# The first batch's convolution and the place of its value products in a fused attention, gated-convolution and spatial-gating kernel

## Chip, cores and metric

One core of one Trainium2 chip runs the whole program in one launch. The metric is the device time of that launch in microseconds. Three runs of the kernel before took 686.89, 687.64 and 688.34 us (median 687.64).

## What is computed

Eight batches of 576 tokens pass through three layers. The core of the reference, shortened:

```python
# attention: 8 heads of 64; plain window of 32, or dilated by 4, in the second half of the heads
scores = np.where(masks, q @ k.T / 8, -1e9)
x = softmax(scores) @ v                       # batch x 576 x 512
...
# gated convolution over time, 5 taps per channel
gate_pre = sum(conv_w[k] * xp[:, k:k + S, :] for k in range(5))
x = (sigmoid(gate_pre) * (x @ w_val)) @ w_out
...
# spatial gating
h = np.maximum(x @ w_in, 0)                   # 512 -> 1024
u, v = h[..., :512], h[..., 512:]
v_s = einsum('ts,bsd->btd', w_spatial, layer_norm(v)) + b_spatial
out = (u * v_s) @ w_out2
```

## The kernel before

Channels lie on partitions, tokens on the free axis. Eight heads are four pairs of two; a pair gives one tile of 128 channels by 576 tokens. The scores of a pair are computed for the 32 by 64 blocks of the band alone (`a_scores`), then come the maximum (`a_max`), the exponentials on ScalarE (`a_exp`), the reciprocal of the sums (`a_sum`), the normalising and turning (`a_trans`), the values (`a_pv`), the convolution (`a_conv`) and its tanh (`a_tanh`). `mlp_steps` holds the rest of a batch: `val` (product with w_val, times the gate), `vstep` (v and its layer norm), `ustep`, `spstep` (spatial product) and `outstep`. The sigmoid is written as half of one plus a tanh.

Two products of weights are taken once: `fuse` multiplies the first layer's w_out (called wm) with the two halves of w_in (wiv for v, wiu for u), so that the middle matrix vanishes. Its products go to PSUM tiles, w_ps in the trace. The weights come as 64-bit words, and `from64` turns them into 32-bit floats with one ScalarE and four VectorE operations (L625, L626, L629, L632, L635). After the first batch most products are done in three passes over a high and a low part of each operand; `split` makes the parts, the high one by a ScalarE cast (L203), the low one by a GpSimd subtraction (L204).

The order of work before the first batch is a list written out by hand, `PRELUDE`. After it, events with places (`FIRST`, `mlp_steps`, `attention_events`) are sorted by place. A scheduler may still reorder within its rules; from the second batch on, TensorE's order is held by `keep_in_program_order`. The engines run their own orders and wait for each other by semaphores.

In the first batch the four pairs go through a path of their own. The block that `a_trans` turns is normalised by four GpSimd multiplications (L350, into `padded`, a part of the tile `boot`), turned by nine TensorE transposes (t_ps, L359) and copied by six ScalarE copies into `pt` (L362). `a_pv` multiplies with the values (o_ps), and ScalarE copies the result to `xt` (L397 or L399). The convolution of pairs 1 to 3 runs on VectorE (L424 and four times L426). That of pair 0 takes the branch at L416: ScalarE scales the five shifted copies (L418, L421), four of them into rotating `spare` tiles, and GpSimd adds them up (L422). ScalarE turns it into the tanh (L433). `val` of the first batch multiplies in one pass of 32-bit floats over four pairs, so each of its eight tiles needs all four `xt`; VectorE takes them out of PSUM (L481) and needs the tanh for that. Four PSUM buffers (`ps_m`) serve t_ps, w_ps and val_ps in turn.

Of the kernel before, what the change touches and what calls it, by code (L numbers as in the profile page):

```python
# [12 lines left out]
ACTF = mybir.ActivationFunctionType  # L13
ALU = mybir.AluOpType
AX = mybir.AxisListType

B, H, S, D = 8, 8, 576, 64
# [4 lines left out]
HS = S // 2  # L22
TAPS = 5
# [65 lines left out]
    ("w_f32", "wv", 1),  # L89
    ("load_w", "wiu", 1),  # L90
    ("a_trans", 0, 1),
    ("a_conv", 0, 0),
    ("fuse", "wiv", 2),
    ("fuse", "wiv", 3),
    ("a_max", 0, 3),
# [3 lines left out]
    ("a_trans", 0, 2),  # L99
    ("a_pv", 0, 2),  # L100
    ("a_trans", 0, 3),
    ("a_pv", 0, 3),
    ("fuse", "wiv", 1),
    ("a_tanh", 0, 0),
    ("a_conv", 0, 1),
    ("a_tanh", 0, 1),
# [40 lines left out]
def _f(ap):  # L147
    return ap.bitcast(F32)
# [3 lines left out]
def attention_gated_mlp_kernel(  # L152
# [15 lines left out]
    nc = tc.nc  # L168
# [13 lines left out]
    cw = const.tile([128, NC, TAPS], F32, name="cw")  # L182
# [6 lines left out]
    held = {}  # L189

    def weight(name):

        if name not in held:
            held[name] = wts.tile(LATE[name], F32R, tag=name, name=name)
        return held[name]

    def spare(name):
        t = rot.tile([128, DM, 2], I32, tag="raw", bufs=4, name=name)
        return _f(t).rearrange("p n w -> p (n w)")

    def split(raw, hi, lo):

        nc.scalar.copy(out=hi, in_=raw)  # L203
        nc.gpsimd.tensor_tensor(out=lo, in0=raw, in1=_f(hi), op=ALU.subtract)  # L204
# [3 lines left out]
    def matmul(o, a, r, start, stop):  # L208

        m = nc.tensor.matmul(o, a, r, start=start, stop=stop)  # L210
        if fixed:
            tc.keep_in_program_order(m)

    def products(o, pairs):
        for i, (a, r) in enumerate(pairs):
            matmul(o, a, r, i == 0, i == len(pairs) - 1)

    def cross(ah, al, bh, bl):
        return [(ah, bh), (ah, bl), (al, bh)]

    def half(i):
        return slice(i * HS, (i + 1) * HS)

    def chunk(c):
        return slice(c * 128, c * 128 + 128)
# [52 lines left out]
    def a_scores(b, p):  # L278
        t = qk_t.pop((b, p))
        s = ps_s.tile([128, 1024], F32, tag="s", name="s_ps")  # L280
        for i in range(2 * NS):
            x, e = divmod(i, 2)
            n = BLOCK[e][x]
            cols = slice(SW * x, SW * x + SW)
            keys = slice(QB * n, QB * n + SW)
            for h in range(2):
                r = slice(64 * h, 64 * h + 64)
                q = t[r, KEYS + QB * n:KEYS + QB * n + QB]
                o = 64 * e + QB * h
                matmul(s[o:o + QB, cols], q, t[r, keys], True, True)  # L290
        if b or p >= 2:
            load_qk(b, p + 2)
        s_t[b, p] = s
# [85 lines left out]
    def a_pv(b, p):  # L379
        u = vv_t.pop((b, p))  # L380
        if b == 0:
            xt = act.tile([128, 4 + S], F32, tag=f"xh{p}", name="xt")
            xh[b, p] = xt[:, 4:]
        else:
            xt = rot.tile([128, 4 + S], F32, tag="xt", name="xt")
        nc.gpsimd.memset(xt[:, 0:4], 0.0)
        o = ps_o.tile([128, 1024], F32, tag="o", name="o_ps")
        for j in range(NJ):
            c = 512 * (j // 3) + 96 * (j % 3)
            for h in range(2):  # L390
                r = slice(64 * h, 64 * h + 64)
                matmul(o[r, c:c + 96], u[:, j, r], pt[:, :, h, j], True, True)
        o = o.rearrange("p (a c) -> p a c", a=2)[:, :, 0:HS]
        if b or p >= 2:
            load_vv(b, p + 2)
        if p < 2:
            nc.scalar.copy(out=xt[:, 4:].rearrange("p (a c) -> p a c", a=2), in_=o)  # L397
        else:
            nc.scalar.copy(  # L399
                out=xt[:, 4:].rearrange("p (i a r) -> p a r i", a=2, r=2),  # L400
                in_=o.rearrange("p a (r i) -> p a r i", r=2),
            )
        x_t[b, p] = xt
# [8 lines left out]
    def a_conv(b, p):  # L412
        xt = x_t.pop((b, p))
        t = act.tile([128, S], F32, tag=f"tt{p}", name="tt")
        tt[b, p] = t
        if b == 0 and p == 0:  # L416

            nc.scalar.activation(out=t, in_=xt[:, 0:S], func=ACTF.Copy, scale=cw[:, p, 0:1])  # L418
            for k in range(1, TAPS):
                u = spare("tap")[:, 0:S]  # L420
                nc.scalar.activation(out=u, in_=xt[:, k:k + S], func=ACTF.Copy, scale=cw[:, p, k:k + 1])  # L421
                nc.gpsimd.tensor_tensor(out=t, in0=t, in1=u, op=ALU.add)  # L422
            return
        nc.vector.tensor_scalar(out=t, in0=xt[:, 0:S], scalar1=cw[:, p, 0:1], scalar2=None, op0=ALU.mult)  # L424
        for k in range(1, TAPS):
            nc.vector.scalar_tensor_tensor(  # L426
                out=t, in0=xt[:, k:k + S], scalar=cw[:, p, k:k + 1], in1=t, op0=ALU.mult, op1=ALU.add
            )
# [31 lines left out]
    def mlp_steps(b):  # L460
# [3 lines left out]
        def val(c, hf):  # L464
            if hf == 0:
                gh[c] = act.tile([128, S + 64], F32R, tag=f"gh{c}", name="gh")
                if c == 0:
                    low["g"] = act.tile([128, NC, S], F32R, tag="gl", name="gl")
            gl = low["g"][:, c]
            ps = ps_m.tile([128, 512], F32, tag="m", name="val_ps")  # L470
            cs, h = chunk(c), half(hf)
            pairs = []
            for e in range(NC):
                if b == 0:
                    pairs.append((wide["wv"][:, e, cs], xh[b, e][:, h]))
                else:
                    wh, wl = weight("wval_h")[:, e, cs], weight("wval_l")[:, e, cs]
                    pairs += cross(wh, wl, xh[b, e][:, h], xl[b][:, e, h])
            products(ps[:, 0:HS], pairs)
            t = tt[b, c][:, h]  # L480
            nc.vector.scalar_tensor_tensor(  # L481
                out=t, in0=t, scalar=1.0, in1=ps[:, 0:HS], op0=ALU.add, op1=ALU.mult
            )
            split(t, gh[c][:, h], gl[:, h])
            if hf == 1:
                nc.gpsimd.tensor_tensor(
                    out=gh[c][:, S:S + 64], in0=t[:, HS - 64:HS], in1=_f(gh[c][:, 512:S]), op=ALU.subtract
                )
# [93 lines left out]

        tiles = [(c, hf) for hf in range(2) for c in range(NC)]
        steps = [(val, c, hf) for c, hf in tiles] + [(vstep, i) for i in range(5)]
        for fn in (ustep, spstep, outstep):
            steps += [(fn, c, hf) for c, hf in tiles]
# [113 lines left out]
    def fuse(key, e):  # L700
# [28 lines left out]
        for fn in (  # L729
            load_qk, load_vv, load_mask, load_ident, load_bias, load_conv_w, load_w, load_sp, conv_w_f32, w_f32,  # L730
            split_pair, split_out, split_sp, fuse, a_scores, a_max, a_exp, a_sum, a_trans, a_pv, a_conv, a_tanh,
        )
    }
# [97 lines left out]
```

## Time and profile before

| | us |
|---|---|
| median of 3 runs | 687.64 (686.89 to 688.34) |
| the profiled execution | 686.94 |
| its span | 685.2 |
| TensorE busy in the span | 654.6 (96%) |
| VectorE busy | 437.1 (64%) |
| ScalarE busy | 291.4 (43%) |
| GpSimd busy | 331.3 (48%) |

The span is what the profiler saw of the program, 1.74 us less than the execution's own time. PE is TensorE's matmul, PEld its weight load, DVE VectorE, ACT ScalarE, POOL GpSimd, SPq the queue on which SyncE issues transfers. Times in the trace are us from the span's start. In a timeline a row gives the start, the length of a run of like instructions, the engine, the line and the tiles; in brackets stands how long the engine had been idle and which engine's work ended that. Matmuls of 32-bit floats appear as two passes each.

### The profile page before, as it was taken

The page shows a single profiled execution, that of the slowest core. Times are in us where ns is not written, and L with a number is a line of the kernel's source. Part 1 is how long each engine was busy: PE and PEld are TensorE (multiplying, and loading weights), DVE is VectorE, ACT ScalarE, POOL GpSimd, SP SyncE. Part 2 cuts the span into 40 slices and gives each one's busy share as a digit, 9 for nine tenths or more (in the row PEclk, how much of TensorE's full clock was granted, in tenths as well). Part 3 has the DMA queues.
Part 4 walks back from the last instruction along what each step waited for, and adds up shares of the span by engine and source line. Part 5 has one row for each costly group of instructions (what it writes and reads, how often), then busy time and mean ns, then how long its engine had stood idle before and what let it go on. Part 6 is the DMA issues. An engine that isn't in the chain of part 4 may idle for free.

```text
span 685.2 us, 16752 instructions
## 1 busy us (share of the span) xinstructions
PE 654.6 (96%) x6804; PEld 599.1 (87%) x6804; DVE 437.1 (64%) x744; ACT 291.4 (43%) x619; POOL 331.3 (48%) x370
## 2 busy tenths in 40 slices
PE   3699889989999999999999999999999999999998
PEld 3456668879899998999899998999899989999998
DVE  5998977984786566656686566656676477632510
ACT  4865356533353334443353334343444334442422
POOL 2675798473544355434545355343635255424420
PEclk9999999999999999999999999999999999999999
DMA  8960124422222431233222421233122411010002
GB/s 338 397 208 28 48 79 146 127 81 92 77 75 78 134 88 31 76 107 110 60 77 77 140 83 54 68 103 115 41 78 85 139 42 33 20 60 18 1 1 70
DMA packets 43553, 63.13 MB, mean 92 GB/s; under 512 B 16850, under 2 KB 32594, under 8 KB 42964
## 3 DMA queue, kind: packets, MB, share of 16 engines
q1 hardware_dynamic: 34260, 52.62, 24.3%
q10 hardware_dynamic: 9216, 9.44, 4.0%
q8 instruction: 54, 0.88, 0.6%
q14 instruction: 23, 0.19, 0.1%
HBM read 44.33 MB, written 9.44 MB: 78 GB/s over the span
## 4 chain that ended last, share of the span: by engine, by line
PE 75%; DVE 12%; POOL 4%; ACT 3%; issue 2%; SPq 2%; DMA 2%; DVEq 0%; POOLq 0%; ACTq 0%
PE sp_ps L210 15%; PE out_ps L210 15%; PE val_ps L210 13%; PE v_ps L210 11%; PE u_ps L210 11%; PE o_ps L210 4%; PE s_ps L210 4%; DVE tt L426 3%; SPq L377 1%; POOL boot L350 1%; POOL vl L537 1%; POOL tt L422 1%; DMA raw<-in_w_mid_t 1%; DVE mx L307 1%; DMA pt<-et 1%
## 5 line engine op out<-in xcount | busy, mean ns | idle before, releaser
L426 DVE SCALAR_TENSOR_TENSOR tt<-xt,cw,tt 128x576 f32<-128x576 f32 x124 | 124.7, 1006 | 1.3
L210 PE MATMUL sp_ps<-wsp_h,vh 128*128 128x288 f32 x320 | 93.7, 297 | 0.6 <-ACT ru L549 0.6
L204 POOL TENSOR_TENSOR gl<-tt,gh 128x288 fp32r<-128x288 f32 x64 | 57.6, 902 | 66.6 <-ACT gh L203 66.6
L204 POOL TENSOR_TENSOR g2l<-ru,g2h 128x288 fp32r<-128x288 f32 x64 | 53.6, 847 | 64.1 <-ACT g2h L203 64.1
L210 PE MATMUL out_ps<-g2h,wout_h 128*128 128x288 f32 x256 | 76.9, 301 | 2.3 <-DVE ru L568 2.1
L210 PE MATMUL u_ps<-gh,w_h 128*128 128x288 f32 x256 | 76.5, 299 | 0.8 <-ACT v_t L501 0.8
L210 PE MATMUL out_ps<-g2l,wout_h 128*128 128x288 f32 x256 | 75.7, 296 | 0.0
L210 PE MATMUL u_ps<-gl,w_h 128*128 128x288 f32 x256 | 75.5, 295 | 0.0
L210 PE MATMUL u_ps<-gh,w_l 128*128 128x288 f32 x256 | 75.5, 295 | 0.0
L210 PE MATMUL sp_ps<-wsp_l,vh 128*128 128x288 f32 x256 | 75.4, 294 | 0.0
L210 PE MATMUL sp_ps<-wsp_h,vl 128*128 128x288 f32 x256 | 75.4, 294 | 0.0
L210 PE MATMUL out_ps<-g2h,wout_l 128*128 128x288 f32 x256 | 74.9, 295 | 0.0
L204 POOL TENSOR_TENSOR xl<-xt,xh 128x576 fp32r<-128x576 f32 x28 | 50.3, 1796 | 48.2 <-ACT xh L203 48.2
L537 POOL TENSOR_TENSOR vl<-v_t,vh 128x512 fp32r<-128x512 f32 x32 | 41.4, 1294 | 52.2 <-ACT vh L528 52.2
L210 PE MATMUL val_ps<-xh,wval_h 128*128 128x288 f32 x224 | 66.5, 297 | 0.0
L210 PE MATMUL val_ps<-xh,wval_l 128*128 128x288 f32 x224 | 66.1, 295 | 0.0
L210 PE MATMUL val_ps<-xl,wval_h 128*128 128x288 f32 x224 | 65.9, 294 | 0.0
L210 PEld LDWEIGHTS sp_ps<-wsp_h,vh 128*128 128x128 f32 x320 | 60.1, 188 | 1.5 <-ACT ru L549 0.9
L210 PE MATMUL v_ps<-w_h,gh 128*128 128x512 f32 x160 | 59.8, 398 | 0.0
L210 PE MATMUL v_ps<-w_l,gh 128*128 128x512 f32 x160 | 59.2, 394 | 0.0
L203 ACT CAST gh<-tt 128x288 fp32r<-128x288 f32 x64 | 27.3, 429 | 74.0 <-DVE tt L481 72.9
L424 DVE TENSOR_SCALAR tt<-xt,cw 128x576 f32<-128x576 f32 x31 | 18.7, 605 | 60.6 <-ACT xt L399 50.2
(137 smaller groups left out, 1666.3 us busy)
## 6 DMA issues: line engine op xcount, KB each, us to landing
qk_t<-in_qk SPq DMA_DIRECT2D x30, 592.0 KB, 4.9
vv_t<-in_vv SPq DMA_DIRECT2D x30, 384.0 KB, 3.9
out<-ob ACTq DMA_DIRECT2D x64, 144.0 KB, 1.8
pt<-et SPq DMA_DIRECT2D x224, 24.0 KB, 1.8
raw<-in_w_in SPq DMA_DIRECT2D x4, 1024.0 KB, 8.0
pt<-et SPq DMA_DIRECT2D x224, 12.0 KB, 1.8
raw<-in_w_mid_t SPq DMA_DIRECT2D x2, 1024.0 KB, 6.0
raw<-in_w_val SPq DMA_DIRECT2D x2, 1024.0 KB, 13.8
```

The lines of the kernel that those rows point to most:

```text
L203: nc.scalar.copy(out=hi, in_=raw)
L204: nc.gpsimd.tensor_tensor(out=lo, in0=raw, in1=_f(hi), op=ALU.subtract)
L210: m = nc.tensor.matmul(o, a, r, start=start, stop=stop)
L307: nc.vector.tensor_reduce(out=mx[:, :, 0], in_=e, axis=AX.X, op=ALU.max)
L350: nc.gpsimd.tensor_tensor(out=padded[r, lo:hi, k:k + SW], in0=e[r, lo:hi], in1=sm[r, lo:hi].to_broadcast([64, hi - lo, SW]), op=ALU.mult,)
L377: nc.sync.dma_start(out=pt[k:k + 32, i, h, j:j + hi - lo], in_=t[r:r + 32, c, lo:hi])
L422: nc.gpsimd.tensor_tensor(out=t, in0=t, in1=u, op=ALU.add)
L424: nc.vector.tensor_scalar(out=t, in0=xt[:, 0:S], scalar1=cw[:, p, 0:1], scalar2=None, op0=ALU.mult)
L426: nc.vector.scalar_tensor_tensor(out=t, in0=xt[:, k:k + S], scalar=cw[:, p, k:k + 1], in1=t, op0=ALU.mult, op1=ALU.add)
L537: nc.gpsimd.tensor_tensor(out=low["v"][:, i], in0=v, in1=_f(h), op=ALU.subtract)
```

## The change

Three things. The call of `a_conv` for pair 0 of the first batch moves in `PRELUDE` from behind the second pair's transposes to behind the last pair's values, and the branch for ScalarE and GpSimd is gone, so that pair 0 is convolved on VectorE like the others. The last part of the fuse that serves v (`fuse` of wiv, 1) moves ahead of the last pair's values. And the first matmul of the first batch's first `val` tile is held in program order, behind the last pair's values. Line numbers behind the edit differ: what was L350 is L353, L424 and L426 are L419 and L421, L715 is L711.

```diff
@@ PRELUDE
     ("a_trans", 0, 1),
-    ("a_conv", 0, 0),
     ("fuse", "wiv", 2),
...
     ("a_trans", 0, 3),
+    ("fuse", "wiv", 1),
     ("a_pv", 0, 3),
-    ("fuse", "wiv", 1),
+    ("a_conv", 0, 0),
     ("a_tanh", 0, 0),
@@ matmul, products
+        return m
-    def products(o, pairs):
+    def products(o, pairs, held=False):
         for i, (a, r) in enumerate(pairs):
-            matmul(o, a, r, i == 0, i == len(pairs) - 1)
+            m = matmul(o, a, r, i == 0, i == len(pairs) - 1)
+            if held and i == 0:
+                tc.keep_in_program_order(m)
@@ a_conv
-        if b == 0 and p == 0:
-
-            nc.scalar.activation(out=t, in_=xt[:, 0:S], func=ACTF.Copy, scale=cw[:, p, 0:1])
-            for k in range(1, TAPS):
-                u = spare("tap")[:, 0:S]
-                nc.scalar.activation(out=u, in_=xt[:, k:k + S], func=ACTF.Copy, scale=cw[:, p, k:k + 1])
-                nc.gpsimd.tensor_tensor(out=t, in0=t, in1=u, op=ALU.add)
-            return
@@ val
-            products(ps[:, 0:HS], pairs)
+
+            products(ps[:, 0:HS], pairs, held=b == 0 and c == 0 and hf == 0)
```

The built programs show what this makes of each engine's order. On TensorE, at the end of the fuse for v (w_ps), the last pair's values (o_ps) and the first batch's products (val_ps), the difference reads:

```order
 L210 MATMUL w_ps<-wiv_f_116,wm_f_264 128x512 x4
-L210 MATMUL val_ps<-xt,wv_f_206 128x288 x6
 L210 MATMUL o_ps<-pt,qkv 64x96 x12
-L210 MATMUL val_ps<-xt,wv_f_206 128x288 x22
+L210 MATMUL val_ps<-xt,wv_f_206 128x288 x28
 L210 MATMUL s_ps<-qk_t 32x64 x36
```

Six products that stood between the fuse and the last values now stand behind the values, with the other 22.

On ScalarE, at the same place, between the last copies into `pt` and the last pair's `xt`, the order before:

```order
L362 COPY pt<-t_ps 128x2x96 x6
L433 ACTIVATE tt<-tt 128x576
L625 ACTIVATE wiu_f_688<-raw 128x1024 x2
L714 ACTIVATE w_h<-w_ps 128x512
L203 CAST wm_h<-wm_f_264 128x512 x4
L433 ACTIVATE tt<-tt 128x576
L399 COPY xt<-o_ps 128x4x144
```

and the order now:

```order
L365 COPY pt<-t_ps 128x2x96 x6
L621 ACTIVATE wiu_f_680<-raw 128x1024
L428 ACTIVATE tt<-tt 128x576
L710 ACTIVATE w_h<-w_ps 128x512
L203 CAST wm_h<-wm_f_264 128x512 x4
L621 ACTIVATE wiu_f_680<-raw 128x1024
L402 COPY xt<-o_ps 128x4x144
```

One of the two conversions of wiu and the tanh of pair 2 have changed sides of the four casts of wm, and that tanh now stands behind the copy of `xt`; the evacuation of the fuse and the casts are ahead of the copy in both.

On VectorE, from the sum of pair 2 (sm) into the maximum of pair 3 (mx) and the conversion of w_val (wv_f), the order before:

```order
L335 TENSOR_SCALAR sm<-sm 128x9
L635 SCALAR_TENSOR_TENSOR wiv_f_116<-raw,wiv_f_116 128x1024
L336 RECIPROCAL sm<-sm 128x9
L303 TENSOR_TENSOR e_t<-s_ps,mask_sb 128x576
L307 TENSOR_REDUCE mx<-e_t 128x9
L309 TENSOR_SCALAR mx<-mx 128x9
L626 TENSOR_SCALAR wv_f_206<-wv_f_206 128x2x512
L629 TENSOR_SCALAR wv_f_206<-wv_f_206 128x2x512
L632 SCALAR_TENSOR_TENSOR wv_f_206<-raw,wv_f_206 128x2x512
L715 SCALAR_TENSOR_TENSOR w_l<-w_ps,w_h 128x512
```

and the order now:

```order
L338 TENSOR_SCALAR sm<-sm 128x9
L419 TENSOR_SCALAR tt<-xt,cw 128x576
L631 SCALAR_TENSOR_TENSOR wiv_f_116<-raw,wiv_f_116 128x1024
L339 RECIPROCAL sm<-sm 128x9
L306 TENSOR_TENSOR e_t<-s_ps,mask_sb 128x576
L421 SCALAR_TENSOR_TENSOR tt<-xt,cw,tt 128x576
L622 TENSOR_SCALAR wv_f_206<-wv_f_206 128x2x512
L310 TENSOR_REDUCE mx<-e_t 128x9
L421 SCALAR_TENSOR_TENSOR tt<-xt,cw,tt 128x576
L625 TENSOR_SCALAR wv_f_206<-wv_f_206 128x2x512
L312 TENSOR_SCALAR mx<-mx 128x9
L622 TENSOR_SCALAR wv_f_206<-wv_f_206 128x2x512
```

The five operations of pair 0's convolution are dealt out among these, three of them here and two more ahead of the reciprocal of pair 3.

On GpSimd, where the first batch's products are split (gl, gh) and the second batch's first pair is normalised (e_t), the order before:

```order
L204 TENSOR_TENSOR gl<-tt,gh 128x288
L486 TENSOR_TENSOR gh<-tt,gh 128x64
L338 TENSOR_TENSOR e_t<-e_t,sm 128x576
L204 TENSOR_TENSOR wiu_l<-wiu_f_688,wiu_h 128x512 x2
L204 TENSOR_TENSOR gl<-tt,gh 128x288
```

and the order now:

```order
L482 TENSOR_TENSOR gh<-tt,gh 128x64
L204 TENSOR_TENSOR wiu_l<-wiu_f_680,wiu_h 128x512
L341 TENSOR_TENSOR e_t<-e_t,sm 128x576
L204 TENSOR_TENSOR wiu_l<-wiu_f_680,wiu_h 128x512
L204 TENSOR_TENSOR gl<-tt,gh 128x288
```

One of the two subtractions of wiu now stands ahead of that normalisation, and one subtraction gl has gone behind both.

## Rows read from the trace of the kernel before

**Rows 1.** Windows: stretch, its length, busy us (instructions) by engine, TensorE's granted clock, DMA.

```profile
26.00:44.00 18.00, 14.19 (x133) 7.75 (x130) 17.83 (x18) 13.14 (x39) 12.75 (x10) 0.91 0.62 231
66.00:90.00 24.00, 20.18 (x216) 15.04 (x215) 19.28 (x30) 7.48 (x15) 18.38 (x19) 1.00 0.18 52
90.00:150.00 60.00, 55.64 (x572) 48.71 (x571) 52.70 (x83) 32.64 (x63) 43.24 (x38) 1.00 0.33 101
150.00:686.00 536.00, 531.35 (x5456) 504.05 (x5455) 311.04 (x560) 208.72 (x414) 236.72 (x277) 1.00 0.24 73
```

**Rows 2.** Timeline of TensorE: the last part of the fuse, products, last values.

```profile
50.27 3.60 PE L210 MATMUL w_ps<-wiv_f,wm_f 128*128 128x512 f32 x8
53.71 3.07 PE L210 MATMUL val_ps<-xt,wv_f 128*128 128x288 f32 x12
56.71 1.21 PE L210 MATMUL o_ps<-pt,qkv 128*64 128x96 f32 x24
```

**Rows 3.** Timeline of VectorE: the convolutions of pairs 1, 2 and 3.

```profile
46.75 1.06 DVE L424 TENSOR_SCALAR tt<-xt,cw 128x576 f32<-128x576 f32 x1
47.85 3.96 DVE L426 SCALAR_TENSOR_TENSOR tt<-xt,cw,tt 128x576 f32<-128x576 f32 x4
51.73 0.52 DVE L424 TENSOR_SCALAR tt<-xt,cw 128x576 f32<-128x576 f32 x1
52.28 3.38 DVE L426 SCALAR_TENSOR_TENSOR tt<-xt,cw,tt 128x576 f32<-128x576 f32 x4
...
59.22 0.60 DVE L424 TENSOR_SCALAR tt<-xt,cw 128x576 f32<-128x576 f32 x1 [2.96 <-ACT xt L399]
```

**Rows 4.** Timeline of ScalarE: taps of pair 0, then what surrounds the last copy.

```profile
27.54 2.76 ACT L421 ACTIVATE tap<-xt,cw 128x576 f32<-128x576 f32 x4
...
52.44 2.18 ACT L625 ACTIVATE wiu_f<-raw 128x1024 f32<-128x1024 f32 x2
54.52 0.58 ACT L714 ACTIVATE w_h<-w_ps 128x512 fp32r<-128x512 f32 x1
55.00 2.16 ACT L203 CAST wm_h<-wm_f 128x512 fp32r<-128x512 f32 x4
...
57.97 1.21 ACT L399 COPY xt<-o_ps 128x576 f32<-128x576 f32 x1 [0.22 <-PE o_ps L210]
...
73.74 1.15 ACT L203 CAST wiu_h<-wiu_f 128x512 fp32r<-128x512 f32 x2 [0.70 <-DVE wiu_f L635]
```

**Rows 5.** Tile wv_f (ns min/median/max, first and last start), then VectorE's timeline.

```profile
L626 DVE TENSOR_SCALAR wv_f<-wv_f x2: 685/1288/1890, 33.8 to 39.5; 128x1024 f32<-128x1024 f32 x2
L629 DVE TENSOR_SCALAR wv_f<-wv_f x2: 881/1328/1775, 34.5 to 41.4; 128x1024 int32<-128x1024 int32 x2
L632 DVE SCALAR_TENSOR_TENSOR wv_f<-raw,wv_f x2: 1224/1482/1739, 35.5 to 43.2; 128x1024 int32<-128x1024 int32 x2
L635 DVE SCALAR_TENSOR_TENSOR wv_f<-raw,wv_f x2: 1165/1498/1832, 37.7 to 45.1; 128x1024 int32<-128x1024 int32 x2
...
28.50 2.42 DVE L632 SCALAR_TENSOR_TENSOR wiv_f<-raw,wiv_f 128x1024 int32<-128x1024 int32 x1
...
44.95 0.20 DVE L336 RECIPROCAL sm<-sm 128x9 f32<-128x9 f32 x1
```

**Rows 6.** Timeline of GpSimd: pair 0's additions, multiplications of pair 2, the next batch.

```profile
28.44 1.40 POOL L422 TENSOR_TENSOR tt<-tt,tap 128x576 f32<-128x576 f32 x1 [0.95 <-ACT tap L421]
32.45 3.66 POOL L350 TENSOR_TENSOR boot<-e_t,sm 64x384 f32<-64x384 f32 x4 [2.61 <-DVE sm L336]
36.19 6.43 POOL L422 TENSOR_TENSOR tt<-tt,tap 128x576 f32<-128x576 f32 x3
...
74.73 1.15 POOL L338 TENSOR_TENSOR e_t<-e_t,sm 128x576 f32<-128x576 f32 x1
75.84 2.53 POOL L204 TENSOR_TENSOR wiu_l<-wiu_f,wiu_h 128x512 fp32r<-128x512 f32 x2
```

**Rows 7.** Waits of TensorE from 50 us on: us in total, times, longest.

```profile
PE w_ps L210 <- POOL wiu_l L204: 2.4, 2, 1.7
```

## The prediction, made before the changed kernel was run

> **What bounds the kernel now.** I read the windows first, because a gain is worth what it is worth where it falls. From 150 us to the end TensorE stands still for only 4.65 of 536 us [rows 1]: work that reaches that part on time cannot shorten it. Before it TensorE waits for others: 3.82 us in 66 to 90 and 4.36 us in 90 to 150. In 26 to 44 us, where the change puts its work, VectorE is busy 17.83 of 18.00 us [rows 1], so that stretch is VectorE's. So the time of the kernel is the time at which the first batch is let into TensorE's full part, and every term below is a shift of that moment.
>
> Then the timelines around the two edits. TensorE ends the fuse at 53.87, does 3.07 us of first products, and only then the last pair's values (o_ps, 56.71) [rows 2]. ScalarE copies these at 57.97, and VectorE, idle for 2.96 us, begins the last convolution at 59.22 [rows 3, 4]. That looks like a wait that the tie removes; term 2 shows why it mostly is not.
>
> **Term 1, the convolution of pair 0.** Out go five ScalarE operations (the four taps take 2.76 us [rows 4], under VectorE's stretch, so worth nothing) and four GpSimd additions. In come one tensor-scalar and four scalar-tensor-tensor operations on VectorE.
> *In:* pair 2's convolution, with GpSimd idle beside it, takes 0.52 + 3.38 = 3.9 us; pair 1's, beside GpSimd, 1.06 + 3.96 = 5.0 us [rows 3]. These are the ends.
> *Out:* while the additions run, VectorE's own operations are stretched. The conversion of wiv took 2.42 us beside the first addition [rows 5, 6]; the same operation on wv has a minimum of 1.22. Beside the other three (36.19 to 42.62 [rows 6]) the conversions of wv go from 0.69 to 1.89, 0.88 to 1.78 and 1.17 to 1.83 [rows 5]. The excess is 1.20 + 1.21 + 0.89 + 0.67 = 4.0 us. The fourth wv operation, 1.74 against 1.22, stands half beside the multiplications of pair 2, so 4.5 is the upper end.
> *Beside the multiplications:* these (32.45, 3.66 us [rows 6]) now meet pieces of the convolution. Between 3.9 and 5.0 I take half, +0.55: pair 1 has a similar four of them beside it, but here a PSUM read and a reduction stand among the pieces.
> *Order:* an operation that needs the one just before it starts 0.03 us after its end (51.73 + 0.52 to 52.28); an independent one 0.08 us before the end (47.85 + 3.96 to 51.73) [rows 3]. The pieces are now dealt out among the conversions and the maximum: nine neighbours stop depending on each other (four in the convolution, five in front), 9 x 0.11 = 1.0 us back; the lower end is none.
> Sum: 3.9 + 0.55 - 4.0 - 1.0 = -0.55 us, with ends of 5.0 - 4.0 = +1.0 and 3.9 - 4.5 - 1.0 = -1.6. This moves pair 3's reciprocal, today at 44.95 [rows 5], which lets GpSimd normalise the last pair, then TensorE transpose it and do the last fuse: all of the first batch hangs on it. The maximum of pair 3 itself comes later, since three pieces stand ahead of it; its exponentials on ScalarE then fall into time that ScalarE spends waiting, and end before the sum is wanted.
>
> The Trainium skill speaks against this edit: "Perfetto Trace Analysis", Optimizing Scalar/DVE Operations, advises moving work from a saturated VectorE to ScalarE or GpSimd. By that alone the term would be +3.9. The same section warns that GpSimd shares a read port with VectorE, and the stretched rows side with the warning.
>
> **Term 2, the tie.** It adds no instruction and no wait, it fixes a place in TensorE's order. The last pair's values leave TensorE 3.07 us earlier after the fuse. But ScalarE is in order, and ahead of their copy its program now has the fuse's evacuation (0.58), four casts of wm (2.16) and one of the two wiu conversions (2.18 for two) [rows 4], the casts waiting for the fuse. From the fuse's end at 53.87: 0.1 + 0.5 + 2.1 + 1.05 = 57.6 to 57.7 against 57.97 today, -0.3 us. So 2.8 of the 3.07 us are hidden behind ScalarE, and VectorE's idle time, 2.96 us, largely stays. The products lose nothing: the same passes run on TensorE, and their first evacuation still waits for the last convolution.
>
> **Term 3, what moves behind.** Together the last convolution begins 0.85 us earlier. Then GpSimd's order differs: one subtraction wiu_l (2.53 / 2 = 1.27 us) goes ahead of the normalisation e_t of the next batch's first pair [rows 6]. It must wait for its cast: today the first of two ends at 73.74 + 0.58 = 74.3 [rows 4]; one short evacuation of the products now stands behind the conversion instead of ahead of it, so about 74.0, and e_t starts near 75.25, not at 74.73: +0.5 on the chain over the transposed block, SP's sixteen small transfers and VectorE. For TensorE the same swap is a gain: its waits for wiu_l, 2.4 us in two [rows 7], lose about a third each way, 0.4 to 0.9. VectorE's chain comes out at -0.85 + 0.5 = -0.35, TensorE's own at about -1.2; what lies between 90 and 150 us follows sometimes one and sometimes the other. I take the middle, **-0.8 us**. SP's spatial loads no longer wait for the taps' buffers and go out earlier; the wiu loads wait for the same conversions as before. Both at nothing: the list of waits shows no engine that stands for either transfer in this stretch.
>
> The profiled execution took 686.94 us, so the sum is 686.1; the median of the runs shown is 0.70 above it, so I forecast **686.8**. Ends: the two of term 1 give 688.4 and 685.8 by the same sum. A measurement of this kernel tells about 0.2% (1.4 us) from no change.
>
> **Rivals.**
> 1. *TensorE's waits go as well (faster).* The statistics of the first v row and the wiu subtractions come earlier in the program. If all of the 2.4 us for wiu_l [rows 7] vanishes, and TensorE is not stopped again before 150, that is 2.4 in place of 0.65: -0.8 - 1.75, about 685.1. For it: 8.2 us of standing between 66 and 150 [rows 1], many chances. Against it: the chain over e_t and SP becomes later, not earlier, and most of the later waits end on VectorE.
> 2. *GpSimd's multiplications hold VectorE for their whole length (slower).* Place: 32 to 36 us. Today beside the four multiplications stand mostly operations that read PSUM or reduce, and VectorE's stretch there is only 0.52 + 0.20 (a tensor-scalar of 0.88 against 0.69). The change deals two tap operations into this place. If each multiplication stops VectorE wholly, the price is 3.66 - 0.72 = 2.9 in place of 0.55: term 1 becomes +1.8, the time 689.2. It decides from a reciprocal of pair 3 at about 46.5. For it: beside the first addition, begun 0.06 us before, VectorE lost 1.20 of the remaining 1.34 us [rows 5, 6]. Against it: the multiplications cover 64 partitions, and pair 1 lost only 1.1 us beside them. The Trainium skill ("SBUF — State Buffer", Who interferes with whom) says that the port pair is an exclusive lock, held for a whole instruction; the first addition agrees with it within 0.14 us.
> 3. *Nothing comes back (slower).* If the stretch in 36 to 43 us had another cause than the additions, all 3.9 us stay: about 690.8. The stretched rows begin and end with the additions, which speaks against it.
> 4. That the tie brings its whole 3.07 us is not a rival: ScalarE's order excludes it unless the casts leave.
>
> **How the numbers follow.** Forecast 0.45, rival 1 0.35, rival 2 0.16, rival 3 0.04. The forecast's own range is 685.8 to 688.4, of which the edge below 686.3 counts as faster, which is in rival 1's chance. The range over all cases reaches from just under rival 1, 684.8, to just over rival 2, 689.4; beyond are stronger forms of rival 1 and rival 3. Faster 0.35, same 0.45, slower 0.20.
>
> **What would show it.** Term 1: the conversions of wv near their minima, pair 3's reciprocal at 44 to 44.8 on VectorE. At 46.5 or later rival 2 holds. Term 2: o_ps directly behind the fuse, yet the copy behind the wm casts near 57.1, and a VectorE wait of 2 to 3 us before the last convolution at 58.4. If that wait is gone, term 2 was wrong. Term 3: e_t of the next batch not earlier than 74.4, and less of TensorE's wait for wiu_l. If TensorE stands less than 6 us between 66 and 150, rival 1 holds. After 150 both traces should take the same time; if not, the whole account is wrong.

## The result and the profile after

The changed kernel took 691.43 us (median of four runs, 690.35 to 692.18) against 687.67 for the kernel before (four runs, 686.89 to 688.34): ratio 1.0051, 95% interval [1.0031, 1.0070]. A second measurement gave 691.42 us and 1.0064 [1.0051, 1.0077]. It is slower, and outside the range of the prediction. The profiled execution took 691.45 us, its span is 689.7; TensorE is busy for 656.7 us, VectorE 440.4, ScalarE 289.6, GpSimd 321.7.

The windows of the changed kernel, for the stretches of [rows 1], and two short ones of 2 us (columns as there):

```profile
26.00:44.00 18.00, 14.66 (x99) 7.18 (x88) 18.00 (x26) 9.93 (x33) 4.85 (x6) 0.81 0.62 234
66.00:90.00 24.00, 19.37 (x213) 14.58 (x211) 18.58 (x30) 6.99 (x14) 16.55 (x19) 0.97 0.13 37
90.00:150.00 60.00, 55.14 (x498) 48.32 (x498) 52.14 (x76) 31.09 (x58) 41.00 (x36) 0.96 0.34 107
150.00:690.00 540.00, 535.10 (x5536) 507.41 (x5535) 315.44 (x568) 212.15 (x419) 239.15 (x281) 1.00 0.24 73
...
32.00:34.00 2.00, 2.00 (x3) 0.67 (x2) 2.00 (x4) 0.00 (x0) 1.93 (x3) 0.50 1.06 402
92.00:94.00 2.00, 2.00 (x6) 1.59 (x5) 1.83 (x4) 1.63 (x4) 1.85 (x2) 0.50 0.51 194
```

Behind 150 us nothing is lost: TensorE stands idle for 4.9 of 540 us, against 4.65 of 536 before. GpSimd lost the 8 us of additions in 26 to 44, as meant. The loss lies between, and one mark shows how much: the first product of the second batch's `val` starts at 161.5 us before and at 166.9 now, 5.4 us later, and from there to the end they need 523.6 and 522.7 us. The windows from 66 us to that mark, of the kernel before:

```profile
66.00:161.50 95.50, 87.23 (x888) 74.49 (x887) 80.08 (x124) 44.62 (x84) 67.29 (x62) 1.00 0.31 96
```

and of the changed kernel:

```profile
66.00:166.90 100.90, 89.96 (x893) 77.06 (x892) 82.90 (x125) 46.02 (x86) 65.62 (x63) 0.97 0.29 90
```

For the same matmuls, bar a few records, TensorE stands idle for 10.94 us in place of 8.27 (+2.7), and is busy for 2.7 us longer, at a granted clock of 0.97 in place of 1.00. So in these two profiles half of the 5.4 us is waiting and half is clock. (The profiled execution of before had a mean clock of 0.998, its other runs mostly 0.993; between medians the clock's part is smaller, see the last section.)

TensorE's timeline after, for [rows 2] (rows between left out):

```profile
31.32 11.79 PE L210 MATMUL w_ps<-wiv_f,wm_f 128*128 128x512 f32 x20 [2.98 <-DVE wiv_f L631]
44.18 0.87 PE L362 MATMUL t_ps<-ident_sb,boot 128*128 128x128 f32 x6
50.68 3.60 PE L210 MATMUL w_ps<-wiv_f,wm_f 128*128 128x512 f32 x8
54.21 1.21 PE L210 MATMUL o_ps<-pt,qkv 128*64 128x96 f32 x24
55.35 8.03 PE L210 MATMUL val_ps<-xt,wv_f 128*128 128x288 f32 x32
87.43 1.22 PE L210 MATMUL w_ps<-wiu_h,wm_h 128*128 128x512 f32 x4 [3.28 <-ACT wiu_h L203]
```

The tie does what it says: the last values (o_ps) follow the fuse at once, at 54.21 in place of 56.71. But the fuse's last part itself begins 0.41 us later than before.

VectorE's timeline after, for [rows 3, 5] and for what follows (rows between left out):

```profile
29.63 0.50 DVE L419 TENSOR_SCALAR tt<-xt,cw 128x576 f32<-128x576 f32 x1
31.93 1.07 DVE L421 SCALAR_TENSOR_TENSOR tt<-xt,cw,tt 128x576 f32<-128x576 f32 x1
34.50 1.19 DVE L421 SCALAR_TENSOR_TENSOR tt<-xt,cw,tt 128x576 f32<-128x576 f32 x1
36.89 0.80 DVE L421 SCALAR_TENSOR_TENSOR tt<-xt,cw,tt 128x576 f32<-128x576 f32 x1
39.95 0.81 DVE L421 SCALAR_TENSOR_TENSOR tt<-xt,cw,tt 128x576 f32<-128x576 f32 x1
43.62 0.20 DVE L339 RECIPROCAL sm<-sm 128x9 f32<-128x9 f32 x1
59.17 0.97 DVE L419 TENSOR_SCALAR tt<-xt,cw 128x576 f32<-128x576 f32 x1 [1.72 <-ACT xt L402]
60.18 4.27 DVE L421 SCALAR_TENSOR_TENSOR tt<-xt,cw,tt 128x576 f32<-128x576 f32 x4
64.37 1.18 DVE L477 SCALAR_TENSOR_TENSOR tt<-tt,val_ps 128x288 f32<-128x288 f32 x3
91.50 0.78 DVE L371 STREAM_TRANSPOSE et<-e_t 128x576 f32<-128x576 f32 x1 [4.65 <-POOL wiu_l L204]
98.32 2.48 DVE L711 SCALAR_TENSOR_TENSOR w_l<-w_ps,w_h 128x512 fp32r<-128x512 f32 x4 [0.37 <-ACT w_h L710]
110.07 0.69 DVE L508 BATCH_NORM_STATS2 st<-v_t 128x6 f32<-128x512 f32 x1 [0.31 <-ACT v_t L497]
```

The tile wv_f after, for the first four lines of [rows 5]:

```profile
L622 DVE TENSOR_SCALAR wv_f<-wv_f x2: 677/835/993, 32.9 to 36.3; 128x1024 f32<-128x1024 f32 x2
L625 DVE TENSOR_SCALAR wv_f<-wv_f x2: 679/680/680, 35.6 to 39.4; 128x1024 int32<-128x1024 int32 x2
L628 DVE SCALAR_TENSOR_TENSOR wv_f<-raw,wv_f x2: 1205/1206/1206, 38.2 to 42.5; 128x1024 int32<-128x1024 int32 x2
L631 DVE SCALAR_TENSOR_TENSOR wv_f<-raw,wv_f x2: 1209/1530/1852, 40.8 to 45.4; 128x1024 int32<-128x1024 int32 x2
```

The five pieces of pair 0's convolution take 0.50 + 1.07 + 1.19 + 0.80 + 0.81 = 4.37 us, the conversions are near their minima, and the reciprocal of pair 3 comes at 43.62 in place of 44.95. ScalarE after, for [rows 4], then GpSimd, for [rows 6] (rows between left out in both):

```profile
54.81 2.17 ACT L203 CAST wm_h<-wm_f 128x512 fp32r<-128x512 f32 x4
57.93 1.21 ACT L402 COPY xt<-o_ps 128x576 f32<-128x576 f32 x1
74.96 1.15 ACT L203 CAST wiu_h<-wiu_f 128x512 fp32r<-128x512 f32 x2 [1.98 <-DVE wiu_f L631]
```

```profile
31.56 3.51 POOL L353 TENSOR_TENSOR boot<-e_t,sm 64x384 f32<-64x384 f32 x4 [4.15 <-DVE sm L339]
45.29 4.63 POOL L353 TENSOR_TENSOR boot<-e_t,sm 64x384 f32<-64x384 f32 x4 [10.22 <-ACT pt L365]
75.66 1.30 POOL L204 TENSOR_TENSOR wiu_l<-wiu_f,wiu_h 128x512 fp32r<-128x512 f32 x1 [0.55 <-ACT wiu_h L203]
76.91 1.16 POOL L341 TENSOR_TENSOR e_t<-e_t,sm 128x576 f32<-128x576 f32 x1
```

GpSimd's second row is the one to look at: pair 3's multiplications wait 10.22 us, and not for the sum (the reciprocal ended at 43.82). The profile names ScalarE's copies into `pt`; these wait for pair 2's transposes (t_ps above, the first six done at 45.05), and the same transposes read the buffer that the multiplications overwrite. The row in the kernel before:

```profile
45.32 4.16 POOL L350 TENSOR_TENSOR boot<-e_t,sm 64x192 f32<-64x192 f32 x4 [2.70 <-ACT pt L362]
```

And the normalisation e_t of the next batch starts at 76.91 in place of 74.73. TensorE's list of waits from 50 us on:

```profile
PE w_ps L210 <- ACT wiu_h L203: 3.3, 1, 3.3
PE o_ps L210 <- DMA pt<-et: 3.0, 3, 2.2
```

The waits for wiu_l [rows 7] are gone; these two stand in their place.

### The profile page after: what moved, and what is told of

It is laid out like the page before. It is cut to its first block, busy times and chain, and to the rows that moved or that the text cites. A ratio compares the mean times of both kernels' runs of the same rounds, so it can differ in the third digit from the quotient of the medians.

```text
span 689.7 us, 16743 instructions
## 1 busy us (share of the span) xinstructions
PE 656.7 (95%) x6804; PEld 601.2 (87%) x6804; DVE 440.4 (64%) x749; ACT 289.6 (42%) x614; POOL 321.7 (47%) x366
## 4 chain that ended last, share of the span: by engine, by line
PE 84%; DVE 8%; ACT 2%; DMA 2%; POOL 2%; issue 1%; SPq 1%; DVEq 0%; POOLq 0%; ACTq 0%
PE sp_ps L210 15%; PE v_ps L210 15%; PE u_ps L210 14%; PE out_ps L210 14%; PE val_ps L210 13%; PE o_ps L210 5%; PE s_ps L210 4%; PE w_ps L210 3%; DVE tt L421 1%; POOL boot L353 1%; DMA raw<-in_w_mid_t 1%; SPq L380 1%; DVE wo_f L628 1%; DMA out<-ob 1%; DMA pt<-et 1%
## 5 line engine op out<-in xcount | busy, mean ns | idle before, releaser
L421 DVE SCALAR_TENSOR_TENSOR tt<-xt,cw,tt 128x576 f32<-128x576 f32 x128 | 130.6, 1022 | 1.2
L204 POOL TENSOR_TENSOR gl<-tt,gh 128x288 fp32r<-128x288 f32 x64 | 56.2, 882 | 68.2 <-ACT gh L203 68.0
L203 ACT CAST g2h<-ru 128x288 fp32r<-128x288 f32 x64 | 27.5, 431 | 70.0 <-DVE ru L564 69.7
```

What stands on the lines that cost most here:

```text
L421: nc.vector.scalar_tensor_tensor(out=t, in0=xt[:, k:k + S], scalar=cw[:, p, k:k + 1], in1=t, op0=ALU.mult, op1=ALU.add)
```

## Experiments

"Theory" in the quoted expectations is the account held when that kernel was run; it changed on the way, from the late normalisation to the order behind it.

### Each edit alone

**e1** leaves the tie out of the changed kernel (without it the fuse's new place in the list alters nothing), so what is left is the convolution on VectorE:

```diff
-            products(ps[:, 0:HS], pairs, held=b == 0 and c == 0 and hf == 0)
+            products(ps[:, 0:HS], pairs)
```

> The kernel before with only the convolution of pair 0 put on VectorE; the order of the fuse, the last values and the first products is that of before. Order theory (the loss comes from the order that the tie makes behind 55 us: the first evacuations after the whole last convolution, and wiu_l ahead of the next batch's normalisation e_t on GpSimd): pair 3's reciprocal near 43.6, e_t of the next batch near 74.5, time 686.9 to 687.9, ratio 0.999 to 1.000. Convolution theory (the five operations on VectorE are not paid back, rival 3 of the prediction): 690.5 to 691.5, ratio 1.004 or more. Clock theory (TensorE's lower granted clock in the fuse, which the earlier start of the fuse causes, costs the time): the fuse again takes about 11.8 us from 31.3, and the time is 688.5 to 690.

**e2** is the kernel before with the fuse ahead of the last values and the tie; pair 0 stays on ScalarE and GpSimd:

```diff
-    ("a_pv", 0, 3),
     ("fuse", "wiv", 1),
+    ("a_pv", 0, 3),
...
+            products(ps[:, 0:HS], pairs, held=b == 0 and c == 0 and hf == 0)
```

> The kernel before with only the fuse's last part ahead of the last values and the first product held behind them; pair 0 is convolved on ScalarE and GpSimd as before. GpSimd's order keeps e_t of the next batch ahead of both wiu_l. Order theory: e_t near 75 and no more, the first evacuations about 1 us later, time 687.5 to 689, ratio 1.000 to 1.002. If the tie costs by itself, whatever GpSimd's order: 690.5 to 691.5, ratio 1.004 or more. Convolution theory: 687.3 to 688, ratio 1.000.

| kernel | median us | ratio to before |
|---|---|---|
| e1, convolution alone | 687.41 | 0.9994 [0.9981, 1.0007] |
| e2, tie alone | 687.49 | 1.0001 [0.9989, 1.0013] |

Neither edit alone costs anything that shows within these intervals; together they cost 0.5 to 0.6%. So it is not VectorE's extra 4.4 us, and not the tie as such. The Trainium skill ("Perfetto Trace Analysis", Optimizing Scalar/DVE Operations) says that moving work from a saturated VectorE to ScalarE or even GpSimd may make sense; by that alone e1, which moves it back, would be slower. The interval says no change, which sides with that section's own warning on the port that GpSimd shares with VectorE.

### The late normalisation and the late copy

**e3** is the changed kernel with e_t held ahead of both subtractions wiu_l on GpSimd:

```diff
+    (4.605, ("split_pair", "wiu", 0)),
...
+            c, s = split(wide[key][:, m, 0:DM], hi, lo)
+            in_order(key == "wiu" and m == 0, s)
```

> The changed kernel with one order restored: on GpSimd the normalisation e_t of the next batch's first pair stands ahead of both subtractions wiu_l, as before. Order theory: e_t starts near 74.5 to 75.3 instead of 76.91, the shift of 2.2 us at e_t shrinks to under 0.7, TensorE's waits for the transposed block and for wiu_h shrink, time 688 to 689.5, ratio to before 1.001 to 1.003. Convolution theory, and late first evacuations alone: nothing comes back, 690.5 to 691.5, ratio 1.004 or more.

**e4** is the changed kernel with the four casts of wm held behind the last pair's copy on ScalarE:

```diff
+    ("split_pair", "wm", 0),
+    ("split_pair", "wm", 1),
...
+            in_order(key == "wm", c)
```

> The changed kernel with ScalarE's four casts of wm held behind the copy of the last pair's xt. On GpSimd e_t stands ahead of both wiu_l here too. Order theory, with term 2 of the prediction (the copy is held by the casts, not by the values): the copy starts near 55.8 instead of 57.93, the last convolution near 57.1 instead of 59.17, the first evacuation near 61.5 to 62.5, e_t near 72.5 to 73.5, time 685.5 to 687, ratio 0.997 to 0.999. Convolution theory: the 2.1 us come off 691.4, about 689.3, ratio 1.002. If another work then bounds the stretch (GpSimd's wm_l, now later), the copy is early and the time stays at 688 or more.

**e5** gives the kernel before what term 3 priced: one wiu_l ahead of e_t. **e9** puts both ahead. **e10** and **e11** do as e5 to the tie alone (e2) and the convolution alone (e1):

```diff
+    (4.59, ("split_one", "wiu", 0)),
+    (4.605, ("split_one", "wiu", 1)),
...
+            in_order(key == "wiu" and m == 1, s)
```

> The kernel before with nothing changed but GpSimd's order at 75 us: one subtraction wiu_l ahead of the next batch's normalisation e_t, the other behind it, as in the changed kernel. Order theory: e_t starts near 76 instead of 74.73 (1.27 us of one wiu_l, less 0.1 of slack), TensorE meets the late transposed block near 90, time 689 to 691, ratio 1.002 to 1.005. If the order at this place costs only its own 1.2 us: 688.5 to 689, ratio 1.0015 to 1.002. If the order is harmless and the changed kernel loses elsewhere: 687 to 688, ratio 1.000.

> As the run with one subtraction wiu_l ahead of the next batch's normalisation in the kernel before, but now both subtractions stand ahead of it: e_t starts near 77.3 instead of 74.73 and the second transposition of that batch near 92.4 to 92.6. If the lateness of e_t is what costs: another 1.2 us over the run with one, 689.5 to 690.5, ratio 1.0035 to 1.005. If the rest of the order that the scheduler makes with the swap costs, and not the lateness: 688.3 to 689.2, as with one, ratio 1.002 to 1.003.

> The tie alone (pair 0 still on ScalarE and GpSimd) with one subtraction wiu_l put ahead of e_t. The tie makes ScalarE's cast wiu_h 1.2 to 1.5 us late, and now e_t has to wait for it: e_t near 77.2 to 77.8. If lateness of e_t costs: 690 to 691.5, ratio 1.004 to 1.0055, with no convolution moved at all. If the changed kernel's loss needs its own order on VectorE behind 90 us: 688.5 to 689.5, ratio 1.002 to 1.003.

> The convolution alone on VectorE, with one subtraction wiu_l put ahead of e_t. wiu_h is not late here: e_t near 75.9. Lateness theory: 688.3 to 689, ratio 1.0015 to 1.0025. If the convolution adds to the loss once the order is disturbed: 690 or more, ratio over 1.004.

**e6** is the changed kernel again, beside e5, e7 and e8. **e7** is e4 with the four subtractions wm_l put off behind the first batch's first subtractions gl, **e8** with them later still:

```diff
+    (2.5, ("low_pair", "wm", 0)),
+    (3.2, ("low_pair", "wm", 1)),
...
+            if key == "wm":
+                in_order(True, nc.scalar.copy(out=hi, in_=wide[key][:, m, 0:DM]))
```

> The changed kernel once more, to see how often its TensorE falls to the lower clock and what that is worth. Order theory: every run is slower than before at the same mean granted clock, median 690.5 to 691.5, ratio 1.004 to 1.006, and runs at a mean clock of 0.995 or more still at 690 or above. Clock theory: the loss sits in the runs at a mean clock of 0.990 or under; runs at 0.995 or more take 687 to 688.5.

> The changed kernel with the casts of wm behind the copy of the last xt, and GpSimd's four subtractions wm_l held among the first subtractions gl instead of beside the last convolution; e_t ahead of both wiu_l. Contention theory (in the run with the copy alone, the convolution begun 3.2 us earlier was stretched from 3.4 to 7.09 us by wm_l): the last convolution takes 3.9 us from 56.0, the first evacuation starts near 60.5 instead of 63.6, and if wm_l then finds room on GpSimd e_t comes near 72 to 73.5 and the time is 685 to 686.5, ratio 0.996 to 0.998. If wm_l stretches the wiu conversions as it stretched the convolution: e_t near 74.5 to 75.5, time 687 to 688.5, ratio 0.999 to 1.001.

> As the run before this one, but wm_l stands still later on GpSimd, two subtractions each behind the sixth and the seventh pair of gl and gh, just ahead of e_t. Contention theory: the last convolution as there, first evacuation near 60.5; e_t then waits for 2.5 us of wm_l, near 74.5 to 76, and TensorE for wm_l near 78: time 687.5 to 690, ratio 1.000 to 1.003, worse than the run before this one by 1 to 3 us.

| kernel | e_t starts | median us | ratio to before |
|---|---|---|---|
| e3, normalisation first | 74.97 | 688.32 | 1.0007 [0.9996, 1.0018] |
| e4, copy first | 74.46 | 688.09 | 1.0006 [0.9992, 1.0019] |
| e5, before, one wiu_l ahead | 76.14 | 688.78 | 1.0023 [1.0014, 1.0032] |
| e9, before, both ahead | 77.28 | 690.06 | 1.0036 [1.0024, 1.0047] |
| e10, tie alone, one ahead | 76.39 | 689.16 | 1.0022 [1.0011, 1.0033] |
| e11, convolution alone, one ahead | 75.59 | 688.48 | 1.0005 [0.9993, 1.0017] |
| e6, changed kernel again | 77.03 | 691.42 | 1.0064 [1.0051, 1.0077] |
| e7, wm_l late | 74.95 | 690.29 | 1.0044 [1.0031, 1.0058] |
| e8, wm_l last | 77.03 | 689.77 | 1.0026 [1.0010, 1.0043] |

e3 and e4 each bring back nearly all of the loss, with e_t early in both; that alone would make the normalisation the culprit. The next rows forbid it. e7 has e_t as early as e3 and still costs 0.44%; e9 has it later than the changed kernel and costs less. And e8, expected to be worse than e7, is better.

Three cautions go with this table. Each start is that of one execution: e3 and e18 below are the same program, and e_t starts at 74.97 in one and at 74.19 in the other. The edit of e5 and e9 is not as small as it looks: counted in the traces as the least number of rows (by operation, tiles and shape) that must move to make one order of the other, the scheduler moved 35 rows of VectorE, 18 of ScalarE and 10 of GpSimd against the kernel before, and 35 or 36 of VectorE in e10 and e11 against e2 and e1. So their 0.05 to 0.36% is not the price of lateness alone; e12 below has that, with all else in e3's order: 0.16%, against 0.07% in e3. And e5 ran at a median granted clock of 0.988, the kernel before at 0.993; at the same clock it is not slower (last section).

e4 and e7 also settle term 2. VectorE's timeline of the last convolution in e4, with GpSimd's wm_l beside it (56.53 to 63.03):

```profile
56.00 0.52 DVE L420 TENSOR_SCALAR tt<-xt,cw 128x576 f32<-128x576 f32 x1 [1.06 <-ACT xt L403]
56.56 7.09 DVE L422 SCALAR_TENSOR_TENSOR tt<-xt,cw,tt 128x576 f32<-128x576 f32 x4
63.57 1.17 DVE L478 SCALAR_TENSOR_TENSOR tt<-tt,val_ps 128x288 f32<-128x288 f32 x3
```

and in e7, with GpSimd idle:

```profile
56.47 3.38 DVE L424 SCALAR_TENSOR_TENSOR tt<-xt,cw,tt 128x576 f32<-128x576 f32 x4
60.41 1.49 DVE L480 SCALAR_TENSOR_TENSOR tt<-tt,val_ps 128x288 f32<-128x288 f32 x3 [0.57 <-PE val_ps L213]
```

With the casts behind it the copy comes at 54.80 in e4, so the casts held it. But 3.7 us of the gain are stretched away again by the four subtractions, and the first evacuation (L478) comes at 63.57, against 63.18 before. The Trainium skill ("SBUF — State Buffer", Who interferes with whom) has VectorE and GpSimd contend for one port pair behind an exclusive lock; 7.09 against 3.38 us agrees that they contend. In e7 the evacuation comes at 60.41, 2.8 us earlier than before, and the kernel is slower all the same: what happens behind 82 us outweighs it.

### VectorE's order behind 82 us

What e7 shares with the changed kernel is VectorE's order there: in the traces 2 rows of VectorE stand elsewhere, while 26 do between the changed kernel and e3. So I wrote that order out as a list of places, forced without adding a wait:

```diff
+ORDER = [
+    89, 90, 91, 92, 102, 93, 99, 103, 94, 100, 104, 95, 101, 112, 113, 114,
...
+    for a, b in zip(ORDER, ORDER[1:]):
+        tc.add_manual_dep(
+            ranked[b], ranked[a].name,
+            mybir.DependencyInfo(mybir.DependencyClass.NoSync, mybir.DependencyReason.DATA),
```

**e12** is the changed kernel, its VectorE in e3's order from about 82 to 155 us; **e13** is e3 with the changed kernel's. The orders of the other engines were left to the scheduler, which moved them too.

> The changed kernel, wiu_l still ahead of e_t on GpSimd, but VectorE's operations from about 82 to 155 us are put into the order of the run e3 (64 places of that stretch differ). e_t near 76.9 as in the changed kernel. If the order on VectorE carries the rest of the loss: 689 to 690, ratio 1.0025 to 1.0035, what a late e_t alone costs. If lateness carries it all: 690.7 to 691.7, ratio 1.005 to 1.006, as in the changed kernel. If TensorE's clock carries it: a mean granted clock of 0.993 with the lower time, or 0.989 with the higher.

> The run e3 (e_t ahead of both wiu_l, near 75), but VectorE's operations from about 82 to 155 us in the order of the changed kernel. If the order on VectorE carries the rest of the loss: 689 to 690, ratio 1.002 to 1.0035, though e_t is early. If lateness carries it all: 688 to 688.6, ratio 1.0005 to 1.0015, as in the run e3.

**e14** to **e17** are e3 with the changed kernel's order in a part only: 82 to 115, behind 116, 82 to 88, and 95 to 115 us, by other lists; e14's part holds those of e16 and e17. **e18** is e3 with its own order written out, to see whether the writing itself costs anything.

> The run e3 with VectorE in the changed kernel's order from 82 to 115 us alone (the wiu conversions, the four evacuations w_l behind the reciprocal, the last taps ahead of the layer norm). If this front part costs: w_l four in a row from about 97.5, the first layer norm behind them near 105 to 106, first u_ps 1.5 to 2.5 us later than in e3, ratio 1.003 to 1.005. If the part behind 116 us costs: ratio 1.0005 to 1.0015.

> The run e3 with VectorE in the changed kernel's order behind 116 us alone (the third conversion of w_out ahead of the second group of evacuations ru). If this part costs: TensorE waits over 2 us more between 137 and 156 us, ratio 1.003 to 1.005. If the front part costs: ratio 1.0005 to 1.0015.

> The run e3 with the changed kernel's order on VectorE only from 82 to 88 us: layer norm of the first v row ahead of the last two wiu conversions, which end some 0.7 us later. If a late wiu_h for the second half of the fuse costs: TensorE's wait for it before 88 us grows by 0.5 to 1 us, ratio 1.0015 to 1.003. If the evacuations w_l cost: ratio 1.0005 to 1.0015.

> The run e3 with the changed kernel's order on VectorE only from 95 to 115 us: the four w_l in a row behind the sum and the reciprocal, the taps ahead of the layer norm. If these evacuations cost (they give TensorE its PSUM buffers back): first u_ps 1 to 2 us later than in e3, ratio 1.0025 to 1.0045. If not: ratio 1.0005 to 1.0015.

> The run e3 once more, with VectorE's order of 82 to 155 us written out as it already was: the same order on every engine. If e3 stands: ratio 1.000 to 1.0018. If its first measurement was lucky: 1.0025 or more, and then the four split runs lie within 0.2% of their base.

| kernel | first evacuation, e_t | median us | ratio to before |
|---|---|---|---|
| e12, changed, e3's order | 63.30, 75.86 | 688.36 | 1.0016 [1.0004, 1.0028] |
| e13, e3, the changed order | 64.86, 76.22 | 691.33 | 1.0047 [1.0032, 1.0062] |
| e14, the same to 115 us only | 63.51, 74.86 | 690.75 | 1.0050 [1.0037, 1.0064] |
| e15, the same behind 116 only | 64.18, 75.54 | 690.20 | 1.0045 [1.0027, 1.0062] |
| e16, the same in 82 to 88 only | 63.00, 74.34 | 689.73 | 1.0038 [1.0026, 1.0051] |
| e17, the same in 95 to 115 only | 62.63, 73.99 | 689.37 | 1.0037 [1.0023, 1.0051] |
| e18, e3 in its own order | 62.84, 74.19 | 687.73 | 1.0007 [0.9995, 1.0018] |

e12, e13 and e14 are the verdict between lateness and order: forcing VectorE's order takes most of the loss away, or brings most of it. e18 shows that forcing an order costs nothing by itself. e_t started at 75.86 in e12, where I had expected 76.9, and at 76.22 in e13, where e3 has 74.97. That came from further ahead, not from the forced rows: from the first evacuation to e_t it is 12.56 us in e12 and 12.54 in the changed kernel, 11.36 in e13 and in e3. e14 has an early e_t, 74.86, and the whole loss. From e_t to the mark of the second batch's `val` the kernel before, e1 to e4, e12 and e18 take 86.8 to 89.1 us, but the changed kernel 90.0 and (e6) 90.9, e13 91.0 and e14 91.5; part of that gap is clock, since the profiled executions of the first group ran at a mean of 0.992 to 0.998 and those of the second at 0.985 to 0.990.

What is not shown is that VectorE's order does it alone. The traces say how far the others went along: e12 is e3 on VectorE and ScalarE, row for row, with one row of GpSimd elsewhere, so 15 rows of ScalarE and 9 of GpSimd came back with VectorE's 26. In e13 VectorE's order is the changed kernel's, but 20 rows of ScalarE and 10 of GpSimd stand elsewhere than in e3, and 15 and 7 elsewhere than in the changed kernel. TensorE's order in the first batch moved too. And the parts don't add up: each of e14 to e17 costs 0.4 to 0.5% by itself. So no single exchange of rows is the whole cause.

What such an order does can be seen at the low parts w_l of the fuse for u. Each of these operations gives TensorE one of its PSUM buffers back. VectorE's timeline in e3:

```profile
89.77 0.78 DVE L373 STREAM_TRANSPOSE et<-e_t 128x576 f32<-128x576 f32 x1 [3.27 <-DMA pt<-et]
...
95.29 0.69 DVE L714 SCALAR_TENSOR_TENSOR w_l<-w_ps,w_h 128x512 fp32r<-128x512 f32 x1
96.19 1.28 DVE L714 SCALAR_TENSOR_TENSOR w_l<-w_ps,w_h 128x512 fp32r<-128x512 f32 x2
97.51 0.63 DVE L714 SCALAR_TENSOR_TENSOR w_l<-w_ps,w_h 128x512 fp32r<-128x512 f32 x1
...
105.75 0.68 DVE L510 BATCH_NORM_STATS2 st<-v_t 128x6 f32<-128x512 f32 x1
```

and in e13:

```profile
90.84 0.78 DVE L384 STREAM_TRANSPOSE et<-e_t 128x576 f32<-128x576 f32 x1 [4.02 <-DMA pt<-et]
...
99.62 2.42 DVE L725 SCALAR_TENSOR_TENSOR w_l<-w_ps,w_h 128x512 fp32r<-128x512 f32 x4
...
110.76 0.69 DVE L521 BATCH_NORM_STATS2 st<-v_t 128x6 f32<-128x512 f32 x1
```

In e3 the four are dealt out as the products come, in e13, as in the changed kernel, they stand in one row behind other work. From the transposition of the block (et) to the layer norm's third statistics e3 takes 105.75 - 89.77 = 15.98 us, before 15.96, e12 15.97; e13 takes 19.92, the changed kernel 110.07 - 91.50 = 18.57. But this stretch is not the whole account either: e18, the same program as e3, takes 17.18 there, at a granted clock of 0.79 in 82 to 90 against e3's 0.89, and e11 takes 18.25 and ends at 1.0005, so a delay can be made up further on.

## Why the prediction was wrong

- **Term 1** was under its forecast, in its favour: the reciprocal moved by 43.62 - 44.95 = -1.33 us, where -0.55 was taken, within the ends. GpSimd's multiplications stretched two pieces by about 0.26 and 0.38 us against the later two, not for their whole length; rival 2 did not come, nor rival 3 (e1). Rival 3's 690.8 lies near the measured time by luck, since its cause is ruled out. What failed here is the step "which lets GpSimd normalise the last pair". The multiplications write `padded`, of which there is one for all pairs and which pair 2's transposes read; on TensorE these stand behind the 20 passes of the fuse, and that stretch took 11.79 us here against 10.24 before, longer at the lower clock (0.50 from 32 to 36 us; before, 0.50 and then 0.73). The first six transposes were done at 45.05 and the multiplications began at 45.29, against 45.32 before, so the 1.33 us bought nothing in this execution. The step itself was read rightly from the trace of before, whatever the bracket there names: the multiplications follow the reciprocal's end (44.95 + 0.20) by 0.17 us, as pair 2's do in the changed kernel (31.39 to 31.56). In e1, e3, e12 and e18, whose fuse ended by 42.6, they follow it by 0.17 to 0.22 us too. What the prediction lacked is the next wait, which here ended as late as the old one.
- **Term 2**: the copy starts at 57.93 against 57.97, -0.04 where -0.3 was taken: the fuse's last part was 0.41 us later. Its mechanism, the casts ahead of the copy, is shown by e4. What it left out is behind the copy: the first evacuation now stands behind all five operations of the last convolution and comes at 64.37, 1.2 us later than before (63.18, ahead of the fifth).
- **Term 3** is the wrong size: e_t is 2.2 us later, where +0.5 was taken: 1.2 us come from the first evacuation, 1.0 from the subtraction wiu_l ahead of it. The cast it waits for was put at "about 74.0" for its end; it started only at 74.96, ScalarE having idled 1.98 us until VectorE's last conversion of wiu (L631) was done. The waits for wiu_l did vanish, as rival 1 had it, but TensorE then waited 3.3 us for wiu_h and 3.0 us for the transfers into `pt`: it stood idle for 9.5 us between 66 and 150, against 8.2, where rival 1 asked for under 6.
- **The step that failed most** is "I take the middle, -0.8 us". It took the chains behind 78 us as following whatever reached them, in the old order. But the scheduler had written another order behind 82 us, on VectorE and with it on the other engines, and e12, e13 and e14 show that this order, not the late arrival, carries most of the loss: 1.0016 with the late e_t in e3's order, 1.0050 with an early one and part of the changed order. The prediction read the order of four engines to about 78 us and priced nothing beyond.
- **What held**: that everything behind 150 us takes the same time, within 0.9 us, so that the kernel's time is the time at which the first batch lets go. The 5.4 us at the mark of the second batch's `val` became 4.5 us of span.

Open is which exchanges in that order matter, since each of four parts of it costs nearly as much as the whole, whether VectorE's rows or those that moved with them on the other engines carry it, and why the scheduler makes this order from the two edits together and from neither alone. No kernel tried beats the one before; the best, e1, can't be told from it.

## What to carry to other kernels

Where a scheduler writes the orders, price the whole difference of the orders, not the rows around the edit: two edits that were free alone cost half a per cent together, most of it in rows 30 us behind them. Before counting an earlier release as a gain, look at what its consumer waits for next; here a buffer came free at 45.05, where the sum had come at 45.15 in the kernel before. And test such a loss by forcing one engine's order onto the other kernel, with a control in its own order, before putting it down to the edit; then count how far the other engines' orders moved with it, because that bounds what the test shows.

## What the runs showed of the hardware

TensorE's granted clock falls to 0.50 (1.2 of 2.4 GHz) in short stretches, most of them around 30 to 38 and 84 to 96 us, and in half of the 20 profiled executions also between 142 and 153. In the changed kernel both rows of 2 us above are at 0.50; before, 32 to 34 is at 0.50 and 92 to 94 at 1.00. Passes of 128x512 are then 0.42 us apart (e3, 90.22 to 90.64) and 0.23 us at the full clock (92.07 to 92.30). Ahead of the drops TensorE had stood for some us (2.98 us before the fuse at 31.32), but a wait alone doesn't decide: before and e3 wait alike ahead of 90 us, 1.46 + 1.71 and 1.74 + 1.72 us, and only e3 drops, to 0.89 in 82 to 90.

Whole executions of one program differ with it. Over 305 executions of 19 kernels, with a level of its own for each kernel, 0.001 less of mean clock goes with 0.30 us more. The changed kernel's median clock is 0.990, the kernel before's 0.993: 0.9 of the 3.9 us go with the clock, 3.0 don't. Executions at one clock say the same: at 0.990 the kernel before took 688.27 to 689.05 us, the changed kernel 691.30 to 691.45. On the same footing e12 lies 0.8 us above the kernel before, e13 1.8, e14 2.4 and the changed kernel 3.0, but e5 and e11 0.2 below it. Whether the changed order brings the drops or only meets them isn't settled.
